# Dividing three PSUM banks differently between transposes and weighted values, in hash-masked attention followed by a mixture of adapters

## The chip, the cores and the metric

The kernel runs on one core of a Trainium2 chip. The core has a matrix engine (TensorE, PE in the profile), three engines for elementwise work (VectorE or DVE, ScalarE or ACT, GpSimd or POOL) and a queue engine for transfers (SyncE or SP). [...] The metric is the time on the device in microseconds (us); less is better.

## The reference

```python
def _attn_ref(q, k, v, proj):                       # q, k, v: (4, 8, 768, 64), proj: (64, 6)
    scale = 1.0 / np.sqrt(D)
    q_bits = (np.einsum('bhsd,dk->bhsk', q, proj) > 0).astype(np.int64)
    k_bits = (np.einsum('bhsd,dk->bhsk', k, proj) > 0).astype(np.int64)
    powers = 2 ** np.arange(n_bits)
    q_bucket = np.sum(q_bits * powers, axis=-1)
    k_bucket = np.sum(k_bits * powers, axis=-1)
    mask = q_bucket[:, :, :, None] == k_bucket[:, :, None, :]
    scores = scale * np.matmul(q, k.transpose(0, 1, 3, 2))
    scores = np.where(mask, scores, -1000000000.0)
    scores = scores - np.max(scores, axis=-1, keepdims=True)
    attn = np.exp(scores)
    attn = attn / (np.sum(attn, axis=-1, keepdims=True) + 1e-09)
    return np.matmul(attn, v)

def _moe_ref(x, w_gate, A, B):                      # x: (3072, 512), 8 experts of rank 16, 2 per row
    logits = x @ w_gate
    topk = np.argpartition(-logits, K, axis=1)[:, :K]
    sel = np.take_along_axis(logits, topk, axis=1)
    sel = sel - sel.max(-1, keepdims=True)
    w = np.exp(sel)
    w /= w.sum(-1, keepdims=True) + 1e-09
    ...
            z = x[mask] @ A[e]
            delta[mask] += w[mask, k, None] * (z @ B[e])
    return x + delta
```

The result of the attention, with its eight heads side by side, is the `x` of the second part.

## The kernel before

**Pairs and slots.** The 32 heads (4 batches of 8) are worked off as 16 pairs of two heads. A pair has 12 times 768 columns of scores of 128 keys each, and these are cut into nine slots of 1,024 columns. In slot s, `score(p, s)` (line 315) computes one group of scores into one of two PSUM buffers of two banks each (`ps_s`), and ScalarE turns it into exponentials in SBUF, P (line 324). This text calls these score s and exp s. The signs of the hash are six more rows of the operands `aug`, so a mask needs no work of its own.

**Order.** Every engine takes its instructions in the order in which the program issues them. That order is written out by hand: `run` (line 587) issues score s of a pair and then, in `pair(p, s)` (line 632), what else belongs to that slot. This work is for three pairs at once:

- For pair p+1 and p+2: `trans` (line 228) brings four 128x128 blocks of q and k into transposed form on TensorE, into a bank of `ps_t`; VectorE (line 244), or ScalarE in some pairs (line 242), copies the bank out to `qkT`. A pair needs three such groups: groups 0 and 1 of pair p+2 in slots 4 and 5 of pair p, group 2 in slot 0 of pair p+1. Behind them GpSimd casts `qkT` to bf16 (`cast`, line 275), and `hash` (line 251) computes the projections on TensorE, again into `ps_t`; VectorE takes their signs (line 260), and SyncE's queue sends these by four small DMAs into `aug` (`sign_dma`, line 163; two of them are issued later, by `hash_b`).
- For pair p-1 and p: `pvmm` (line 333) computes the weighted values, here called pv: six query slices per head, each of six matmuls of 65 columns, all into one bank of `ps_v`. `pv(p,0)` is issued in slots 6, 7 and 8, two slices in each; `pv(p-1,1)` of the pair before in slots 1 and 3, three slices in each. `norm` (line 363) then adds the uniform part that keeps empty buckets defined (line 374), takes the reciprocal of the sums and multiplies (line 379) into `x`; for the second head GpSimd also casts `x` to bf16 (`xb`, line 385). The next pv in the same bank has to wait for that. `uniform` (line 354) computes the uniform part of a pair by one matmul into `ps_t`, copied out by VectorE (line 361). From pair 12 on a matmul with a tiny constant (`eps`, line 340) does this inside the bank of pv.
- `vcast` (line 214) prepares v for pair p+1 on GpSimd. `xturn` (line 443) transposes `xb` by a DMA; in every fourth pair `xtrans` (line 451) does it on TensorE, through a bank of `ps_t`.
- The adapters (MoE) run in `moe_slot` (line 568) from pair 5 on, one to three row slots in a pair: two in pairs 5, 6, 9 and 10, one in pairs 7, 8, 11 and 12, three in 13 and 14. Logits and low-rank products (lz, line 477) come in slots 0 and 1, routing on VectorE in slots 1 to 3, the transpose of the weighted products (`zmtrans`, line 525; its copy zmT is line 534) in slot 4, and `delta` (line 538) from slot 6 on. All of these go through the one bank of `ps_m`.

**Banks.** `ps_s` holds four banks, `ps_t` two, `ps_v` one and `ps_m` one, eight in all. A tile of a pool waits until the tile that had its buffer before has been read for the last time. Some tiles are put into other pools by hand: the second head of pair 14 uses `ps_t` for its pv, and in the last pair, which `last_pair` (line 673) issues in thirds and sixths, `third` and `sixth` alternate between `ps_v` and `ps_t`.

Of the kernel before, what the change touches and what calls it, by code (L numbers as in the profile page):

```python
# [12 lines left out]
F32 = mybir.dt.float32  # L13
# [6 lines left out]
class Emitter:  # L20


    def __init__(self, ctx, tc, q, k, v, proj, w_gate, A, Bm, out):
        self.tc, self.nc = tc, tc.nc
        nc = self.nc
        self.out = out
        B, H, S, D = q.shape
        self.B, self.H, self.S, self.D = B, H, S, D
        self.nbits = proj.shape[1]
        self.E = w_gate.shape[1]  # L30
        self.r = A.shape[2]
        self.Dm = w_gate.shape[0]
        self.P = P = 128
        self.T = S // P
        self.n_pairs = B * H // 2
        self.PPB = H // 2
        self.ER = self.E * self.r
        self.LZ = self.E + self.ER
        T = self.T
        assert (P, T, D, self.nbits, self.Dm, self.ER) == (128, 6, 64, 6, 512, 128)  # L40

        self.nat, self.vn, self.qkT, self.P_, self.pv = {}, {}, {}, {}, {}
        self.x, self.xb, self.xT, self.lz = {}, {}, {}, {}
        self.uni = {}
        self.rt, self.zm, self.zmT, self.acc, self.pvl, self.me, self.gw = {}, {}, {}, {}, {}, {}, {}
        one = lambda n: ctx.enter_context(tc.tile_pool(name=n, bufs=1))
        self.singles = one("singles")
        self.natp = ctx.enter_context(tc.tile_pool(name="natp", bufs=3))
        self.qktp = ctx.enter_context(tc.tile_pool(name="qktp", bufs=2))
        self.sgp = ctx.enter_context(tc.tile_pool(name="sgp", bufs=2))  # L50
        self.pp = ctx.enter_context(tc.tile_pool(name="pp", bufs=2))
        self.xp = ctx.enter_context(tc.tile_pool(name="xp", bufs=2))
        self.accp = ctx.enter_context(tc.tile_pool(name="accp", bufs=3))
        self.smallp = ctx.enter_context(tc.tile_pool(name="smallp", bufs=4))
        ps = lambda n, b: ctx.enter_context(
            tc.tile_pool(name=n, bufs=b, space=bass.MemoryType.PSUM))
        self.ps_s = ps("ps_s", 2)
        self.ps_t = ps("ps_t", 2)
        self.ps_v = ps("ps_v", 1)
        self.ps_m = ps("ps_m", 1)  # L60

        self.q, self.k, self.v, self.proj = q, k, v, proj
        self.w_gate, self.A, self.Bm = w_gate, A, Bm
        self.nD = self.Dm // P


    def prologue(self):
        nc, sg, P, T, D, S = self.nc, self.singles, self.P, self.T, self.D, self.S

        self.pst = sg.tile([P, 6], F32, name="pst")  # L70
        nc.scalar.dma_start(out=self.pst, in_=self.proj.unsqueeze(0).to_broadcast([2, D, 6]))
        nat = self.natp.tile([P, 2, 2, T * D], F32, tag="nat", name="nat0")
        self.nat[0] = nat
        for h in range(2):
            for i, src in enumerate((self.q, self.k)):
                nc.sync.dma_start(out=nat[:, i, h], in_=src[0, h].rearrange("(p t) d -> p (t d)", t=T))
        self.load_qk(1)
        self.load_v(0)

        self.eps = sg.tile([P, P], BF16, name="eps")  # L80
        nc.vector.memset(self.eps, 2.0 ** -56)
        self.ident = sg.tile([P, P], F32, name="ident")
        make_identity(nc, self.ident)
        first = sg.tile([P, 1], F32, name="first")
        nc.scalar.activation(out=first, in_=self.eps[:, 0:1], func=ACT.Exp)
        self.proj2 = sg.tile([P, 32], F32, name="proj2")
        nc.vector.memset(self.proj2, 0.0)

        self.aug = [sg.tile([P, 4, S], BF16, name=f"aug{i}") for i in range(2)]
        for j in range(8):  # L90
            eng = nc.vector if j < 2 else nc.gpsimd
            eng.memset(self.aug[j // 4][64:96, j % 4, :], (1.0, -1.5)[j % 2])
        self.qkT[0] = self.qktp.tile([P, 2 * S], F32, tag="qkT", name="qkT0")
        self.warm(19)
        self.turn0(0, self.ps_s, "s")
        self.half0(0, 0, nc.scalar.copy)
        self.half0(0, 1, nc.scalar.copy)
        self.signs0()
        self.turn0(1, self.ps_t, "t")
        for e in range(2):  # L100
            nc.vector.tensor_copy(out=self.proj2[64 * e:64 * e + 64, e:12:2],
                                  in_=self.pst[64 * e:64 * e + 64, :])
        self.half0(1, 0, nc.gpsimd.tensor_copy)
        self.half0(1, 1, nc.gpsimd.tensor_copy)

        self.vb = []
        for i in range(3):
            a = sg.tile([P, 2, T + 1, D + 1], BF16, name=f"vb{i}")
            nc.gpsimd.memset(a[:, :, 0:T, D:D + 1], 1.0)
            nc.gpsimd.memset(a[:, :, T:T + 1, D:D + 1], float(T))  # L110
            self.vb.append(a)
        self.vcast(0)
        self.ident_bf = sg.tile([P, P], BF16, name="ident_bf")
        nc.gpsimd.tensor_copy(out=self.ident_bf, in_=self.ident)
        self.wa = sg.tile([P, self.nD, self.LZ], BF16, name="wa")
        self.Bcat = sg.tile([self.ER, self.Dm], BF16, name="Bcat")
        self.warm(6)
# [107 lines left out]

    def trans(self, p, g, on_act=False):
        if p >= self.n_pairs:
            return  # L230
        nc, P = self.nc, self.P
        if g == 0:
            self.qkT[p] = self.qktp.tile([P, 2 * self.S], F32, tag="qkT", name=f"qkT{p}")
        ps = self.ps_t.tile([P, 512], F32, tag="t", name=f"tr{p}_{g}")
        for j in range(4):
            idx, u = divmod(4 * g + j, 3)
            nc.tensor.transpose(out=ps[:, j * P:(j + 1) * P],  # L237
                                in_=self.nat[p][:, idx % 2, idx // 2, u * P:(u + 1) * P],
                                identity=self.ident)
        out = self.qkT[p][:, g * 512:(g + 1) * 512]  # L240
        if on_act:
            nc.scalar.mul(out, ps, 2.0 ** -5)
        else:
            nc.vector.tensor_scalar(out=out, in0=ps, scalar1=2.0 ** -5, scalar2=None, op0=ALU.mult)  # L244
# [88 lines left out]
    def pvmm(self, p, h, i0, i1):  # L333
        if p < 0:
            return
        if i0 == 0:
            pool, tag = (self.ps_t, "t") if (p, h) == (self.n_pairs - 2, 1) else (self.ps_v, "v")
            self.pv[p, h] = pool.tile([self.P, self.T, self.D + 1], F32, tag=tag, name=f"pv{p}_{h}")
            if self.uni_pe(p):
                self.nc.tensor.matmul(  # L340
                    out=self.pv[p, h], lhsT=self.eps, start=True, stop=False,
# [46 lines left out]
    def third(self, u, part):  # L388
        nc, P, T, D = self.nc, self.P, self.T, self.D
        p, b = self.n_pairs - 1, self.B - 1  # L390
        if part == 0:
            pool, tag = (self.ps_t, "t") if u == 1 else (self.ps_v, "v")
            pv = pool.tile([P, 2, 2, D + 1], F32, tag=tag, name=f"pvl{u}")
            ri = self.smallp.tile([P, 2, 2], F32, tag="ri", name=f"ril{u}")
            self.pvl[u] = pv, ri
            nc.tensor.matmul(
# [14 lines left out]
    def sixth(self, sl, j0, j1):  # L411
        nc, P, T, D = self.nc, self.P, self.T, self.D
        p, b = self.n_pairs - 1, self.B - 1
        if j0 == 0:
            pool, tag = (self.ps_v, "v") if sl == 4 else (self.ps_t, "t")
            pv = pool.tile([P, 2, D + 1], F32, tag=tag, name=f"pvs{sl}")
            ri = self.smallp.tile([P, 2], F32, tag="ri", name=f"ris{sl}")
            self.pvl[sl] = pv, ri
            nc.tensor.matmul(out=pv, lhsT=self.eps, rhs=self.vb[p % 3][:, :, T, :], start=True, stop=False)
# [183 lines left out]
    def first_pair(self, s):  # L603
# [3 lines left out]
            self.load_v(1)  # L607
            self.load_v(2)
        if s < 3:
            self.trans(1, s)  # L610
        if s == 3:
            self.cast(1, 0)
            self.cast(1, 1)
# [9 lines left out]
            self.trans(2, 0)  # L623
        if s == 7:
            self.pvmm(0, 0, 2, 4)
            self.trans(2, 1)
        if s == 8:
            self.pvmm(0, 0, 4, 6)
            self.load_moe(0)
# [2 lines left out]
    def pair(self, p, s):  # L632
# [2 lines left out]
            self.trans(p + 1, 2)  # L635
            self.load_qk(p + 3, (0,))
        if s == 1:
            self.pvmm(p - 1, 1, 0, 3)
            self.cast(p + 1, 0)
            self.cast(p + 1, 1)  # L640
        if s == 2:
# [2 lines left out]
                self.hash_b(p + 1)  # L644
            self.load_qk(p + 3, (1,))
        if s == 3:
            self.uniform(p)
            self.pvmm(p - 1, 1, 3, 6)
        if s == 4:
            self.norm(p - 1, 1)  # L650
            self.trans(p + 2, 0, on_act=len(self.moe_group(p)[1]) > 1)
        if s == 5:
            if p % self.PPB:
                self.xturn(p - 1)
            if p + 1 < self.n_pairs - 1:
                self.hash_b(p + 1)
            self.vcast(p + 1)
            self.trans(p + 2, 1)
            if p < 4:
                self.load_moe(p + 1)  # L660
            if p == 3:
# [1 line left out]
        if s == 6:  # L663
            self.pvmm(p, 0, 0, 2)
        if s == 7:
            self.pvmm(p, 0, 2, 4)
        if s == 8:
            self.pvmm(p, 0, 4, 6)
            if p % self.PPB == 0:
                self.xtrans(p - 1)  # L670
            self.load_v(p + 3)
# [1 line left out]
    def last_pair(self, p, b):  # L673
# [46 lines left out]
        self.totals(b, t[1])  # L720
        self.delta(b, t[1], 0, by_pool=True)
        self.route_b(b, t[2], sums=False)
        self.zmtrans(b, t[2], on_act=True, bank=one)
        self.sixth_x(5, x)
        self.totals(b, t[2])
        self.delta(b, t[1], 1, by_pool=True)
# [49 lines left out]
```

## Time and profile before

| what | us |
|---|---|
| median of 11 runs | 178.44 (177.79 to 179.54) |
| the profiled execution | 178.51 |
| its span, first to last instruction | 176.7 |

TensorE's granted clock in this execution was 0.983 on average. A pair's length can be read from the starts of its exps. From exp 3 of one pair to exp 3 of the next:

| from pair to pair | adapter slots of the two pairs | us |
|---|---|---|
| 1 to 2, 2 to 3, 3 to 4 | 0, 0 | 8.91, 8.92, 8.92 |
| 4 to 5 | 0, 2 | 9.96 |
| 5 to 6, 9 to 10 | 2, 2 | 9.85, 9.85 |
| 6 to 7, 10 to 11 | 2, 1 | 9.61, 9.61 |
| 7 to 8, 11 to 12 | 1, 1 | 9.71, 9.71 |
| 8 to 9 | 1, 2 | 10.56 |
| 12 to 13 | 1, 3 | 10.25 |
| 13 to 14 | 3, 3 | 10.56 |

Exp 3 of pair 1 starts 22.95 after the first instruction, and exp 3 of pair 14 at 149.34; what comes before and after are the start and the last pair.

How to read the profile's rows: the name on the left of an arrow is written, those on the right are read. On TensorE the rows of matmuls that follow each other overlap, because they are pipelined, and their ends are modelled; how long a step holds the engine is read from its start to the start of the next step. What stands in brackets is the idle time before a row, and the row that ended it.

### The profile page before, as it was taken

The numbers are of one execution on the slowest core, as the hardware profiler recorded it, in microseconds if no ns is written. First come the engines' busy times: TensorE is split into PE (matmuls) and PEld (weight loads), VectorE is DVE, ScalarE is ACT, GpSimd is POOL, SyncE is SP. The second block draws the span as 40 slices with busy tenths as digits, with TensorE's granted clock in tenths as the row PEclk, the third lists the DMA queues.
The fourth block names the chain that finished last, engine by engine and source line by source line (L and its number), as shares of the span: only waits on it lengthen the run. The fifth ranks groups of instructions, "written<-read, shape, count | busy, mean of one in ns | idle before, by whom it ended". The sixth has DMA issues, their size and how long they took to land.

```text
span 176.7 us, 5259 instructions
## 1 busy us (share of the span) xinstructions
PE 162.1 (92%) x2100; PEld 112.7 (64%) x2105; DVE 115.3 (65%) x312; ACT 151.8 (86%) x176; POOL 115.4 (65%) x140
## 2 busy tenths in 40 slices
PE   7989999999999999998989999998999999999750
PEld 6355676767676666666666666666578675687610
DVE  3663674747475686868496686868594776646861
ACT  3578999999999798998998799998999897997760
POOL 8299988787975676666664676666675566620180
PEclk9999999999999999999999999999999999999985
DMA  5936496998997078958864378968965034350036
GB/s 149 344 134 185 153 260 144 170 129 210 121 232 259 5 125 249 192 141 282 137 222 151 111 132 264 171 161 264 131 225 168 4 50 182 41 195 4 2 121 235
DMA packets 30438, 28.51 MB, mean 161 GB/s; under 512 B 15078, under 2 KB 28494, under 8 KB 30414
## 3 DMA queue, kind: packets, MB, share of 16 engines
q1 hardware_dynamic: 25020, 27.38, 58.6%
q0 software_dynamic: 4832, 0.27, 4.6%
q10 hardware_dynamic: 562, 0.53, 0.9%
q8 instruction: 16, 0.26, 0.7%
q14 instruction: 8, 0.07, 0.1%
HBM read 19.42 MB, written 6.29 MB: 145 GB/s over the span
## 4 chain that ended last, share of the span: by engine, by line
PE 69%; DVE 15%; POOL 6%; issue 5%; ACT 2%; DVEq 0%; POOLq 0%; ACTq 0%
PE s L322 27%; PE pv L329 15%; PE tr L237 8%; PE hs L257 7%; PE lz L477 3%; POOL xb L385 2%; PE dl L545 2%; DVE x L379 2%; DVE pv L374 2%; POOL vs L221 2%; DVE sgn L260 2%; DVE zm L510 1%; POOL vb L219 1%; PE warm L184 1%; PE xtp L460 1%
## 5 line engine op out<-in xcount | busy, mean ns | idle before, releaser
L324 ACT ACTIVATE P<-s 128x1024 bf16<-128x1024 f32 x144 | 140.6, 1028 | 12.4 <-PE s L322 11.3
L322 PE MATMUL s<-aug 71*128 71x256 bf16 (+2 forms) x408 | 86.2, 316 | 2.1 <-issue 0.8
L275 POOL CAST aug<-qkT 64x1536 bf16<-64x1536 f32 x30 | 43.8, 1461 | 18.1 <-DVE qkT L244 14.7
L329 PEld LDWEIGHTS <-P 128*128 128x128 bf16 x1080 | 42.1, 97 | 12.5 <-DVE x L379 4.4
L329 PE MATMUL pv<-vb,P 128*128 128x65 bf16 x1080 | 45.2, 194 | 2.7 <-DVE zmT L534 1.7
L322 PEld LDWEIGHTS <-aug 71*128 71x128 bf16 x408 | 33.0, 97 | 21.0 <-issue 10.7
L244 DVE TENSOR_SCALAR qkT<-tr 128x512 f32<-128x512 f32 x40 | 26.9, 682 | 2.3 <-POOL aug L275 1.3
L385 POOL CAST xb<-x 128x768 bf16<-128x768 f32 x15 | 12.3, 822 | 23.5 <-DVE x L379 19.8
L237 PE MATMUL tr<-ident,nat 128*128 128x128 f32 x180 | 27.2, 273 | 0.0
L237 PEld LDWEIGHTS tr<-ident,nat 128*128 128x128 f32 x180 | 21.8, 140 | 4.8 <-issue 0.6
L260 DVE TENSOR_SCALAR sgn<-hs 128x384 bf16<-128x384 f32 x15 | 8.4, 558 | 17.7 <-PE hs L257 16.9
L374 DVE TENSOR_TENSOR pv<-pv,uni 128x390 f32<-128x390 f32 x24 | 13.6, 565 | 9.0 <-PE pv L329 8.7
L553 DVE SCALAR_TENSOR_TENSOR acc<-dl,rt,x 128x512 f32<-128x512 f32 (+1 forms) x21 | 15.0, 720 | 6.7 <-PE dl L545 6.7
L379 DVE TENSOR_TENSOR x<-pv,ri 128x384 f32<-128x384 f32 x30 | 16.7, 557 | 1.0
L221 POOL TENSOR_TENSOR vs<-vn 128x384 f32<-128x384 f32 x16 | 15.9, 992 | 0.0
L219 POOL CAST vb<-vn 128x768 bf16<-128x768 f32 x16 | 13.2, 825 | 0.1
L257 PE MATMUL hs<-qkT,proj 128*32 128x384 f32 x120 | 12.8, 498 | 0.0
L551 POOL TENSOR_TENSOR acc<-tmp,x 128x512 f32<-128x512 f32 x4 | 5.0, 1264 | 8.8 <-ACT tmp L550 8.8
L477 PE MATMUL lz<-wa,xT 128*128 128x136 bf16 x96 | 9.3, 223 | 0.6 <-ACT xT L462 0.6
L545 PE MATMUL dl<-Bcat,zmT 128*128 128x512 bf16 x19 | 7.7, 404 | 1.0 <-ACT zmT L534 0.8
L224 POOL TENSOR_TENSOR vb<-vs,vs 128x128 bf16<-128x128 f32 x16 | 7.3, 457 | 1.3
L223 POOL TENSOR_TENSOR vs<-vs 128x128 f32<-128x128 f32 x16 | 7.3, 454 | 1.3
(73 smaller groups left out, 118.9 us busy)
## 6 DMA issues: line engine op xcount, KB each, us to landing
vn<-in_v_dram SPq DMA_DIRECT2D x16, 384.0 KB
nat<-in_q_dram SPq DMA_DIRECT2D x15, 384.0 KB
nat<-in_k_dram SPq DMA_DIRECT2D x15, 384.0 KB
out_dram<-acc SPq DMA_DIRECT2D x4, 512.0 KB
out_dram<-acc SPq DMA_DIRECT2D x8, 256.0 KB
out_dram<-acc SPq DMA_DIRECT2D x2, 768.0 KB
aug<-sgn SPq DMA_DIRECT2D x60, 9.0 KB
nat<-in_q_dram SPq DMA_DIRECT2D x2, 192.0 KB
```

The costliest lines, as they stand in the source:

```text
L221: nc.gpsimd.tensor_add(out=s3, in0=vn[:, :, 0:3, :], in1=vn[:, :, 3:6, :])
L237: nc.tensor.transpose(out=ps[:, j * P:(j + 1) * P], in_=self.nat[p][:, idx % 2, idx // 2, u * P:(u + 1) * P], identity=self.ident)
L244: nc.vector.tensor_scalar(out=out, in0=ps, scalar1=2.0 ** -5, scalar2=None, op0=ALU.mult)
L257: nc.tensor.matmul(out=ps[32 * j:32 * j + 32, :], lhsT=self.proj2, rhs=self.qkT[p][:, j * 384:(j + 1) * 384], start=True, stop=True)
L275: self.nc.gpsimd.tensor_copy(out=self.aug[p % 2][0:64, :, e * n:(e + 1) * n], in_=self.qkT[p][64 * e:64 * e + 64, :].rearrange("p (j c) -> ...
L322: nc.tensor.matmul(out=ps[:, o:o + n], lhsT=aug[0:71, 2 * h + 1, kt * P:(kt + 1) * P], rhs=q, start=True, stop=True)
L324: nc.scalar.activation(out=self.P_[p][:, s * 1024:(s + 1) * 1024], in_=ps, func=ACT.Exp, scale=128.0)
L329: self.nc.tensor.matmul(out=pv, lhsT=self.p_at(p, h, kt, i), rhs=self.vb[p % 3][:, h, self.slot(kt), :], start=(start and kt == 0), stop=( ...
L374: nc.vector.tensor_tensor(out=pv[:, 0:T, :], in0=pv[:, 0:T, :], in1=self.uni[p][:, h:h + 1, :].to_broadcast([P, T, D + 1]), op=ALU.add)
L379: nc.vector.tensor_tensor(out=self.x[b][:, :, c:c + D].rearrange("p (u e) d -> p e u d", e=2), in0=pv[:, 0:T, 0:D].rearrange("p (e u) d -> ...
L385: nc.gpsimd.tensor_copy(out=self.xb[b][:, hp], in_=self.x[b][:, :, hp * P:(hp + 1) * P])
L553: nc.vector.scalar_tensor_tensor(out=acc[:, i, c], in0=ps[:, c], scalar=self.rt[b, slots][:, i:i + 1], in1=self.x[b][:, slots[i], c], op0= ...
```

## The change

The pools are divided anew: one bank for transposes (`ps_t`), two for weighted values (`ps_v`). Then the work is moved between the slots of a pair:

- pv(p-1,1) in slots 1, 3 and 4, two slices each, in place of slots 1 and 3, three each; pv(p,0) in slots 6, 7 and 8 with two, one and three slices in place of two each.
- `uniform` from slot 3 to slot 4, behind pv; `hash_b` from slot 5 to slot 4; the norm of pv(p-1,1) from slot 4 to slot 5.
- The transposes of groups 0 and 1 from slots 4 and 5 to slots 5 and 7; `xturn` from slot 5 to slot 7.
- In the first pair, which has no adapters yet, three groups of transposes use `ps_m`, and the prologue's second turn uses `ps_v`.
- The tiles that were put into `ps_t` for want of a second bank in `ps_v` are in `ps_v` now, and the last `zmtrans` is in `ps_m`.

What is computed stays the same, and so does the number of instructions of every kind on the compute engines.

```diff
@@ pools
-        self.ps_t = ps("ps_t", 2)
-        self.ps_v = ps("ps_v", 1)
+        self.ps_t = ps("ps_t", 1)
+        self.ps_v = ps("ps_v", 2)
@@ prologue
-        self.turn0(1, self.ps_t, "t")
+        self.turn0(1, self.ps_v, "v")
@@ trans
-    def trans(self, p, g, on_act=False):
+    def trans(self, p, g, on_act=False, bank=None):
...
-        ps = self.ps_t.tile([P, 512], F32, tag="t", name=f"tr{p}_{g}")
+        pool, tag = bank or (self.ps_t, "t")
+        ps = pool.tile([P, 512], F32, tag=tag, name=f"tr{p}_{g}")
@@ pvmm
-            pool, tag = (self.ps_t, "t") if (p, h) == (self.n_pairs - 2, 1) else (self.ps_v, "v")
-            self.pv[p, h] = pool.tile([self.P, self.T, self.D + 1], F32, tag=tag, name=f"pv{p}_{h}")
+            self.pv[p, h] = self.ps_v.tile([self.P, self.T, self.D + 1], F32, tag="v", name=f"pv{p}_{h}")
@@ third
-            pool, tag = (self.ps_t, "t") if u == 1 else (self.ps_v, "v")
-            pv = pool.tile([P, 2, 2, D + 1], F32, tag=tag, name=f"pvl{u}")
+            pv = self.ps_v.tile([P, 2, 2, D + 1], F32, tag="v", name=f"pvl{u}")
@@ sixth
-            pool, tag = (self.ps_v, "v") if sl == 4 else (self.ps_t, "t")
-            pv = pool.tile([P, 2, D + 1], F32, tag=tag, name=f"pvs{sl}")
+            pv = self.ps_v.tile([P, 2, D + 1], F32, tag="v", name=f"pvs{sl}")
@@ first_pair
-            self.trans(1, s)
+            self.trans(1, s, bank=None if s == 1 else (self.ps_m, "m"))
...
-            self.trans(2, 1)
+            self.trans(2, 1, bank=(self.ps_m, "m"))
@@ pair
         if s == 1:
-            self.pvmm(p - 1, 1, 0, 3)
+            self.pvmm(p - 1, 1, 0, 2)
...
         if s == 3:
+            self.pvmm(p - 1, 1, 2, 4)
+        if s == 4:
+            self.pvmm(p - 1, 1, 4, 6)
             self.uniform(p)
-            self.pvmm(p - 1, 1, 3, 6)
-        if s == 4:
-            self.norm(p - 1, 1)
-            self.trans(p + 2, 0, on_act=len(self.moe_group(p)[1]) > 1)
-        if s == 5:
-            if p % self.PPB:
-                self.xturn(p - 1)
             if p + 1 < self.n_pairs - 1:
                 self.hash_b(p + 1)
+        if s == 5:
+            self.norm(p - 1, 1)
             self.vcast(p + 1)
-            self.trans(p + 2, 1)
+            self.trans(p + 2, 0, on_act=len(self.moe_group(p)[1]) > 1)
...
         if s == 7:
-            self.pvmm(p, 0, 2, 4)
+            if p % self.PPB:
+                self.xturn(p - 1)
+            self.trans(p + 2, 1)
+            self.pvmm(p, 0, 2, 3)
         if s == 8:
-            self.pvmm(p, 0, 4, 6)
+            self.pvmm(p, 0, 3, 6)
@@ last_pair
-        self.zmtrans(b, t[2], on_act=True, bank=one)
+        self.zmtrans(b, t[2], on_act=True)
```

## The prediction

> **What bounds the kernel now.** I read the page's first part, then ScalarE's timeline, then TensorE's and VectorE's timelines through single head pairs. The page:
>
> ```profile
> PE 162.1 (92%) x2100; PEld 112.7 (64%) x2105; DVE 115.3 (65%) x312; ACT 151.8 (86%) x176; POOL 115.4 (65%) x140
> L324 ACT ACTIVATE P<-s 128x1024 bf16<-128x1024 f32 x144 | 140.6, 1028 | 12.4 <-PE s L322 11.3
> ```
>
> Exps fill ScalarE; what it waits for is scores. Its timeline (start, length, idle before) shows where:
>
> ```profile
> 31.86 8.62 ACT L324 ACTIVATE P<-s 128x1024 bf16<-128x1024 f32 x9 [0.30 <-PE s L322]
> ...
> 58.33 1.02 ACT L324 ACTIVATE P<-s 128x1024 bf16<-128x1024 f32 x1 [0.78 <-PE s L322]
> ...
> 83.49 5.03 ACT L324 ACTIVATE P<-s 128x1024 bf16<-128x1024 f32 x5 [0.47 <-PE s L322]
> ```
>
> The first is exp 3 of pair 2, behind hash and slot 1's weighted values; the second exp 2 of pair 5; the third exp 7 of pair 7. TensorE's rows, pair 7 and then pair 5's one line:
>
> ```profile
> 77.16 0.60 PE L322 MATMUL s<-aug 71*128 71x256 bf16 x3
> 77.68 0.85 PE L257 MATMUL hs<-qkT,proj 128*32 128x384 f32 x8
> 78.47 0.61 PE L322 MATMUL s<-aug 71*128 71x512 bf16 x3
> 78.91 0.22 PE L359 MATMUL un<-vb,eps 128*128 128x130 bf16 x1
> 78.97 0.71 PE L329 MATMUL pv<-vb,P 128*128 128x65 bf16 x18
> 79.52 0.60 PE L322 MATMUL s<-aug 71*128 71x512 bf16 x2
> 79.95 0.60 PE L237 MATMUL tr<-ident,nat 128*128 128x128 f32 x4
> 80.39 0.22 PE L531 MATMUL ztp<-ident_bf,zm 128*128 128x128 bf16 x1
> 80.45 0.60 PE L322 MATMUL s<-aug 71*128 71x256 bf16 x3
> 80.88 0.60 PE L237 MATMUL tr<-ident,nat 128*128 128x128 f32 x4
> 81.32 0.60 PE L322 MATMUL s<-aug 71*128 71x512 bf16 x3
> 82.49 0.53 PE L329 MATMUL pv<-vb,P 128*128 128x65 bf16 x12 [0.57 <-DVE zmT L534]
> 82.86 0.60 PE L322 MATMUL s<-aug 71*128 71x512 bf16 x2
> ...
> 56.90 0.72 PE L329 MATMUL pv<-vb,P 128*128 128x65 bf16 x18 [0.41 <-DVE x L379]
> ```
>
> Rows overlap, so a step's cost is start to next start: score 0.44 (0.52 ahead of the hash), hash 0.79, four transposes 0.44, 18 weighted-value matmuls 0.55 (0.183 a query slice), 12 of them 0.37, uniform 0.06, one adapter transpose 0.06. Likewise, elsewhere: logits of one slot 0.24, delta 0.22, the six bf16 transposes 0.33, an eps matmul (pairs 12 up) 0.17. Nearly no gap is left: a pair without MoE takes 8.92 us from exp 3 to exp 3, with 0.44 of TensorE waiting. [...] The starts allow 0.44; I follow them.
>
> **Rules of my sums**, all from rows: an exp starts 0.64 after its score, and 0.91 after the exp before at the earliest; score s+2 starts 0.05 after exp s ends (score 0: 0.26), an exp lasting 1.02 to 1.05. Walking the old order of a pair without MoE by these gives 8.9; the trace has 8.92.
>
> **Part 1, weighted values get two banks.** Slot 1's pv(p-1,1) no longer waits for norm(p-1,0) to empty the one bank: 0.31 in pair 1, 0.57 in pairs 5 and 9 (starts 55.89 to 56.90, less 0.44). With one bank, norm(p-1,1) had to be over before slot 6; now it may come later.
>
> **Part 2, norm(p-1,1) in slot 5 behind the adapter copy zmT.** Delta at slot 6 waits for zmT, which VectorE runs behind that norm (0.59+0.23+0.47=1.3) and a transpose copy (0.60). By starts the stall is 0.52 in pairs 7, 8, 11 (81.32 to 82.49, less score 0.44 and delta 0.22), 0.27 in pair 12, 0.20 in the two-slot pairs 5, 6, 9, 10. In the new order zmT follows the uniform copy directly, 0.8 before delta needs it: all gone. Moved with norm, on POOL: the xb cast (0.82) and vcast (2.7) behind it, about a slot later, ending near 7.3 after score 3 (8.2 in pairs 1 to 3, with load_moe's 0.9); the casts behind them wait for slot 0's transposes until about 7.9 anyway. If that cover went, a late cast would first meet score 0 of the next pair, nine slots on.
>
> **Part 3, 2+2+2 and 2+1+3.** One slice (0.18) leaves the stretch before the hash; 24 matmuls instead of 18 follow it, where a slot has 0.91 and score+pv needs 0.81. Uniform in slot 4 is behind them.
>
> **Part 4, SP.** hash_b's two sign DMAs (0.8 each to issue) go from slot 5 to 4, the DMA transpose (1.26) from slot 5 to 7, past them, behind it the vn load. The signs are needed at score 4 of the next pair, xT at the tightest behind score 5 of the last pair, seven slots later: cost zero. xT's landing has no row; between 0 and, if it took more than those 6 us, the excess. I take 0.
>
> **Part 5, one bank for transposes, hash, uniform, xtrans.** This adds waits; all PE work queues behind them. [...] Walk of pair 7, score 3 at 0: pv 0.44, score 0.81, pv 1.25, uniform 1.61, adapter transpose 1.67, score 5 1.73, transposes 2.16, score 6 2.63 (waits for exp 4), delta 3.07, pv 3.28, score 7 3.65. VectorE: uniform copy 1.87 (0.26 after its matmul, as 78.91 to 79.17), zmT 2.08, norm 2.21, transpose copy 3.52 to 4.20. Slot 7's transposes, ready at 4.09, start at 4.23: **wait 0.14**. Then pv 4.67, score 8 4.85, pv 5.29, score 0 5.84, transposes 6.27, logits 6.71, score 1 6.95, pv 7.38, score 2 7.75, hash 8.28, score 3 **9.06**; the old interval is 9.71.
> Cost bounds of that wait: 0 (copy on ScalarE, as in pairs 5, 6, 9, 10, 13) to 0.74 (one delta op of VectorE ahead); a wait gains nothing; the rows above give 0.11 to 0.14, which I take.
> xtrans in pairs 4, 8, 12: its copy ends 1.09 after its first matmul (54.45 to 55.54), the next transposes are due at 0.77: **wait 0.35** each. In pair 12 no norm wait goes in exchange (that norm lacks the add), so it loses.
> Pair 0: uniform directly behind the hash now waits for the sign copy (end 15.63, and 0.05): 15.68 against 14.93, **0.75**. Slack further on (pair 1's 0.31 wait, its slice) leaves 0.24.
>
> **The other walks**, score 3 at 0, by the same costs. *No MoE*: score 5 1.72, score 6 2.63, score 7 3.55, transposes due 3.99 and held to 4.10, score 8 4.72, pv 5.16, score 0 5.71, score 1 6.58, pv 7.02, score 2 held by exp 0 to 7.42, hash 7.95, score 3 8.74. *4 to 5*: the same to 5.71, then xtrans, score 0 6.04, transposes held to 6.83, logits 7.27, score 1 7.50, pv 7.94, logits 8.31, score 2 8.54, hash 9.07, score 3 9.86. *8 to 9*: pair 7's walk to 5.84, then as 4 to 5: 9.98. *Two slots*: score 5 1.78, score 6 2.65, delta 3.09, pv 3.30, score 7 3.67, transposes 4.10 (copy on ScalarE, no wait), pv 4.54, delta 4.72, score 8 4.95, pv 5.38, score 0 held by exp 7 to 6.07, transposes 6.50, logits 6.94, score 1 7.18, pv 7.61, logits 7.98, score 2 8.21, hash 8.74, score 3 9.53; into a one-slot pair one logits group less, 9.29. *12 to 13*, with eps, xtrans and three logits groups: 10.42. *13 to 14*: delta's waits for its own bank stay, 10.46.
>
> **Sum**, old minus new from exp 3 to exp 3: start to pair 1 -0.24; three without MoE, 8.92 to 8.74, +0.54; 4 to 5, 9.96 to 9.86, +0.10; 5 to 6 and 9 to 10, 9.85 to 9.53, +0.64; 6 to 7 and 10 to 11, 9.61 to 9.29, +0.64; 7 to 8 and 11 to 12, 9.71 to 9.06, +1.30; 8 to 9, 10.56 to 9.98, +0.58; 12 to 13, 10.25 to 10.42, -0.17; 13 to 14, +0.10; pair 14 to score 0 of pair 15 (no transposes; zmT early again, a stall of 0.36) +0.37. Last pair: its pv tiles alternated between two banks and still do; zmtrans goes to ps_m, emptied by a copy over 1 us earlier (ScalarE, 168.49, for a transpose at 169.89): 0.
> Total 3.9. The walks forget small jitters; I take 3.8: the profiled execution's 178.51 becomes **174.7**. It lies 0.07 above the median of the runs, 178.44.
>
> **Rivals.** *Only the named waits go*: if slot 7, now 0.44+0.18+0.22 beside the score, lets no slice gain through, there remain pair 1, 5, 9 (0.31+2×0.57), zmT (3×0.52+0.27+4×0.20+0.36), less 3×0.35 and 0.75: 2.6, so 175.9. For it: in two-slot pairs TensorE waits just 0.45 of 9.85. Against: slots 3 to 5 got lighter. *Slower*: the slot 7 transposes wait on VectorE behind norm. The mechanism decides from 0.3 more per pair over 13 pairs, 3.9. If a delta op of 0.74 stood before the slot 5 copy in the eight pairs 5 to 12 and jitter put 0.2 on the rest, 6 to 7 us go: 181. Against it: that copy comes before delta in VectorE's order. *Hidden anyway*: ScalarE's pace and the hash stretch (score 0.52, hash 0.79, score 0.64, after 1.08 for an exp: 3.03 of exp 0 to exp 3's 3.2) swallow it: 178.4.
>
> **Chances.** Forecast 0.60, named waits only 0.19, hidden 0.08, slower 0.13. Range 173.5 to 178.1: below, the walk's 3.9 with both 0.35 and 0.75 waits half as large; above, four fifths reach it. Within 0.3% (0.5 us) is what no change looks like. Faster 0.79, same 0.07, slower 0.14.
>
> **What would show it.** Right: no DVE zmT and no DVE x ahead of weighted values on TensorE; exp 3's idle of 0.30 near 0.12; exp 7's 0.47 gone; new waits of about 0.1 before slot 7's transposes on VectorE's copy, 0.35 behind xtrans, 0.7 in pair 0. Wrong: transposes waiting over 0.4 in every pair, or delta in slot 7 waiting for its bank.

## The result and the profile after

| | before | after |
|---|---|---|
| median (runs) | 178.50 (47) | 176.34 (12, 175.46 to 178.73) |
| the profiled execution | 178.51 | 176.48 |
| its span | 176.7 | 174.7 |

The ratio after to before is 0.9875, with a 95% interval of 0.9853 to 0.9898: the change saves about 2.2 us in the medians and 2.03 between the two profiled executions. The forecast was 3.8, so little more than half of it came. The ratio is taken over executions within 1.5% of the fastest; two of the twelve after, at 178.60 and 178.73, are left out of it.

The page of the kernel after, its first part, and its groups for exps, weighted values and transposes (busy time and mean of one, idle time before them and what ended it); the last two rows are those of before for weighted values and transposes. Line numbers differ from those of before by up to two.

```profile
PE 162.2 (93%) x2100; PEld 112.1 (64%) x2105; DVE 116.1 (66%) x312; ACT 150.7 (86%) x176; POOL 115.4 (66%) x140
L325 ACT ACTIVATE P<-s 128x1024 bf16<-128x1024 f32 x144 | 139.7, 1030 | 11.6 <-PE s L323 10.0
L330 PE MATMUL pv<-vb,P 128*128 128x65 bf16 x1080 | 47.5, 194 | 0.2
L238 PEld LDWEIGHTS tr<-ident,nat 128*128 128x128 f32 x180 | 20.2, 140 | 10.0 <-DVE qkT L245 3.1
...
L329 PE MATMUL pv<-vb,P 128*128 128x65 bf16 x1080 | 45.2, 194 | 2.7 <-DVE zmT L534 1.7 <-DVE x L379 1.0
L237 PEld LDWEIGHTS tr<-ident,nat 128*128 128x128 f32 x180 | 21.8, 140 | 4.8 <-issue 0.6
```

ScalarE's wait for scores fell from 11.3 to 10.0. The weighted values wait for nothing any more (0.2 in all, where 2.7 stood before). The transposes now wait, as announced, on VectorE's copies of the one bank; the wait shows at the weight load (PEld), which comes first. Its 10.0 is not lost time of TensorE as it stands: the matmuls of these transposes had 0.6 of idle before them. ScalarE's timeline at the places that answer to those shown of before (start, length, idle before):

```profile
32.50 8.69 ACT L325 ACTIVATE P<-s 128x1024 bf16<-128x1024 f32 x9 [0.17 <-PE s L323]
...
57.88 2.07 ACT L325 ACTIVATE P<-s 128x1024 bf16<-128x1024 f32 x2 [0.46 <-PE s L323]
...
79.09 4.74 ACT L325 ACTIVATE P<-s 128x1024 bf16<-128x1024 f32 x5
84.00 4.03 ACT L325 ACTIVATE P<-s 128x1024 bf16<-128x1024 f32 x4 [0.17 <-PE s L323]
```

Exp 3 of pair 2 has 0.17 of idle ahead of it instead of 0.30. The 0.46 ahead of exp 1 of pair 5 is the wait behind xtrans; the 0.78 ahead of exp 2 is gone. From exp 3 of pair 7 five exps run without a gap, and exp 7's 0.47 is gone; ahead of exp 8 there is a new 0.17, behind slot 7's transposes. TensorE's timeline of pair 7, and then two weight loads of transposes and the uniform's copy:

```profile
78.44 0.61 PE L323 MATMUL s<-aug 71*128 71x512 bf16 x3
78.89 0.53 PE L330 MATMUL pv<-vb,P 128*128 128x65 bf16 x12
79.26 0.60 PE L323 MATMUL s<-aug 71*128 71x512 bf16 x2
79.69 0.53 PE L330 MATMUL pv<-vb,P 128*128 128x65 bf16 x12
80.06 0.22 PE L359 MATMUL un<-vb,eps 128*128 128x130 bf16 x1
80.12 0.22 PE L529 MATMUL ztp<-ident_bf,zm 128*128 128x128 bf16 x1
80.17 0.60 PE L323 MATMUL s<-aug 71*128 71x256 bf16 x3
80.67 0.66 PE L238 MATMUL tr<-ident,nat 128*128 128x128 f32 x4
81.16 0.60 PE L323 MATMUL s<-aug 71*128 71x512 bf16 x3
81.81 0.53 PE L330 MATMUL pv<-vb,P 128*128 128x65 bf16 x12
82.18 0.60 PE L323 MATMUL s<-aug 71*128 71x512 bf16 x2
82.69 0.66 PE L238 MATMUL tr<-ident,nat 128*128 128x128 f32 x4
...
80.32 0.29 DVE L361 COPY uni<-un 128x130 f32<-128x130 f32 x1 [0.46 <-PE un L359]
80.66 0.42 PEld L238 LDWEIGHTS tr<-ident,nat 128*128 128x128 f32 x4 [0.28 <-DVE uni L361]
84.68 0.47 PEld L238 LDWEIGHTS tr<-ident,nat 128*128 128x128 f32 x4
```

Up to score 5 (1.73 after score 3) this is the walk of the prediction to 0.01. Then slot 5's transposes start 0.50 behind it (80.17 to 80.67) instead of 0.44, and last 0.49 to the next score (80.67 to 81.16) instead of 0.44: they waited 0.06 for the uniform's copy (it ends at 80.61, just when they are due), and four transposes that start after a wait take 0.055 longer (the *restart*). The weight loads fit that: after the wait the first starts with the transposes (80.66 and 80.67), while ahead of slot 0's transposes at 84.79, which take 0.44, it starts 0.11 earlier. So score 6 starts 2.72 after score 3, where the walk had 2.63. Slot 7's transposes, ready at 82.62, start at 82.69 and again take 0.49. Delta in slot 6 has no matmul record here, but from score 6 to pv there are 0.65, its own 0.22 and the score's 0.44, so nothing waits there. The intervals from exp 3 to exp 3:

| from pair to pair | before | forecast | after |
|---|---|---|---|
| start to 1 | 22.95 | 23.19 | 23.20 |
| 1 to 2 | 8.91 | 8.74 | **9.31** |
| 2 to 3, 3 to 4 | 8.92, 8.92 | 8.74 | 8.86, 8.87 |
| 4 to 5 | 9.96 | 9.86 | 10.02 |
| 5 to 6, 9 to 10 | 9.85 | 9.53 | 9.54 |
| 6 to 7, 10 to 11 | 9.61 | 9.29 | 9.30 |
| 7 to 8, 11 to 12 | 9.71 | 9.06 | 9.14 |
| 8 to 9 | 10.56 | 9.98 | 10.15 |
| 12 to 13 | 10.25 | 10.42 | 10.50 |
| 13 to 14 | 10.56 | 10.46 | 10.74 |
| 14 to 15 | 9.18 | 8.81 | 8.93 |
| 15 to the end | 18.19 | 18.19 | 18.17 |

The first row agrees by luck in part: exp 0 of pair 0 starts at 9.01 before and 8.96 after, and anywhere from 8.20 to 9.32 in the profiles of this study. From there to exp 3 of pair 1 the change took 0.30 more, where 0.24 was forecast. The two waits that were forecast on a single user of the bank, first in pair 0 (the second two rows are before), then behind xtrans:

```profile
14.04 0.85 PE L258 MATMUL hs<-qkT,proj 128*32 128x384 f32 x8
15.57 0.23 PE L359 MATMUL un<-vb,eps 128*128 128x130 bf16 x1 [0.68 <-DVE sgn L261]
...
14.15 0.85 PE L257 MATMUL hs<-qkT,proj 128*32 128x384 f32 x8
14.93 0.23 PE L359 MATMUL un<-vb,eps 128*128 128x130 bf16 x1
...
55.70 0.60 PE L323 MATMUL s<-aug 71*128 71x512 bf16 x3
56.52 0.66 PE L238 MATMUL tr<-ident,nat 128*128 128x128 f32 x4 [0.22 <-DVE xT L460]
```

### The profile page after: what moved, and what is told of

Same layout as the page of the kernel before. It is cut to its first block, busy times and chain, and to the rows that moved or that the text cites. A ratio compares the mean times of both kernels' runs of the same rounds, so it can differ in the third digit from the quotient of the medians.

```text
span 174.7 us, 5249 instructions
## 1 busy us (share of the span) xinstructions
PE 162.2 (93%) x2100; PEld 112.1 (64%) x2105; DVE 116.1 (66%) x312; ACT 150.7 (86%) x176; POOL 115.4 (66%) x140
## 3 DMA queue, kind: packets, MB, share of 16 engines
q0 software_dynamic: 4832, 0.27, 4.7%
## 4 chain that ended last, share of the span: by engine, by line
PE 79%; DVE 7%; POOL 5%; issue 3%; ACT 2%; POOLq 1%; ACTq 0%; DVEq 0%
PE s L323 32%; PE pv L330 17%; PE tr L238 12%; PE hs L258 7%; PE lz L475 4%; PE dl L543 1%; POOL xb L385 1%; PE warm L184 1%; PE xtp L458 1%; DVE xT L460 1%; POOL vs L221 1%; ACT P L325 1%; PE trf L125 1%; POOL vb L219 1%; PE hsd L139 1%
## 5 line engine op out<-in xcount | busy, mean ns | idle before, releaser
L330 PEld LDWEIGHTS <-P 128*128 128x128 bf16 x1080 | 44.9, 98 | 11.3
L330 PE MATMUL pv<-vb,P 128*128 128x65 bf16 x1080 | 47.5, 194 | 0.2
L245 DVE TENSOR_SCALAR qkT<-tr 128x512 f32<-128x512 f32 x40 | 27.5, 686 | 8.9 <-PE tr L238 8.4
L238 PE MATMUL tr<-ident,nat 128*128 128x128 f32 x180 | 28.3, 280 | 0.6 <-DVE xT L460 0.6
L238 PEld LDWEIGHTS tr<-ident,nat 128*128 128x128 f32 x180 | 20.2, 140 | 10.0 <-DVE qkT L245 3.1
L543 PE MATMUL dl<-Bcat,zmT 128*128 128x512 bf16 x19 | 7.2, 381 | 1.1 <-ACT zmT L532 0.8
L361 DVE COPY uni<-un 128x130 f32<-128x130 f32 x12 | 3.5, 294 | 7.2 <-PE un L359 7.2
```

Source lines behind the costliest of these rows:

```text
L238: nc.tensor.transpose(out=ps[:, j * P:(j + 1) * P], in_=self.nat[p][:, idx % 2, idx // 2, u * P:(u + 1) * P], identity=self.ident)
L330: self.nc.tensor.matmul(out=pv, lhsT=self.p_at(p, h, kt, i), rhs=self.vb[p % 3][:, h, self.slot(kt), :], start=(start and kt == 0), stop=( ...
```

## The experiments

Theory: the walk, that is the prediction's sum of steps along a pair. Two banks for weighted values and the later norm take waits away, one bank for transposes adds some, and each shows in the interval of its pairs. Rivals: only one half of the change matters, or the smaller pieces alone give the gain. The experiments start from the kernel after unless it says otherwise.

**The two halves alone.** `banks_only` has the new banks with the body of `pair` of before; `order_only` the new order with the banks of before (`ps_t` 2, `ps_v` 1, and the tiles that were put into other pools). The edits in short:

```diff
 banks_only: pools, prologue, first_pair, third, sixth as in after
-    def pair(self, p, s):        # after
+    def pair(self, p, s):        # before
 order_only: pair as in after
-        self.ps_t = ps("ps_t", 1)
+        self.ps_t = ps("ps_t", 2)
-        self.ps_v = ps("ps_v", 2)
+        self.ps_v = ps("ps_v", 1)
```

> The new banks with the old order of a pair's slots. Walk theory (the two halves need each other): uniform stands right behind the hash and waits about 0.3 us for the sign copy, group 1's transposes in slot 5 wait 0.5 us for group 0's copy behind the norm in the pairs where VectorE makes it, and zmT keeps its place behind the norm; against that only the waits of 0.3 and twice 0.57 for pv's bank go. Slower than before: 180 to 183 us. Rival (the second bank for weighted values brings the gain, the order only repairs the transposes): 176.5 to 178 us.

> The new order with the old banks (two for transposes, one for weighted values). Walk theory: pv(p,0) in slot 6 must now wait for the norm issued in slot 5, 0.2 to 0.4 us in every pair, and pv(p,1) in slot 1 for the norm of slot 0; zmT's stalls stay gone. 177.5 to 180 us, on TensorE a wait for DVE x ahead of pv in nearly every pair. Rival (the order alone brings the gain, and one bank for pv is enough): 175.5 to 176.5 us, since the waits on the single transpose bank are gone too.

Measured: `banks_only` 193.67, ratio 1.082 (1.073 to 1.091); `order_only` 179.61, ratio 1.007 (1.004 to 1.010). Neither half gives a gain. A group of `banks_only` (transposes) and one of `order_only` (weighted values):

```profile
L238 PE MATMUL tr<-ident,nat 128*128 128x128 f32 x180 | 29.0, 284 | 10.9 <-DVE qkT L245 7.2 <-ACT qkT L243 3.0 <-DVE xT L460 0.6
```

```profile
L330 PE MATMUL pv<-vb,P 128*128 128x65 bf16 x1080 | 47.7, 194 | 5.0 <-DVE x L380 5.0
```

With one bank and transposes in neighbouring slots TensorE stands 10.9 us before them; a pair without MoE takes 10.11 to 10.12. I had the direction and a fifth of the size. (In two of its four executions, the profiled one among them, 1 to 2 us more go with a halved clock, which is told of at the end; the fastest took 192.00.) With the new order and one bank for weighted values these wait 5.0 us for norm, which now comes a slot later. The two halves only work together.

**The norm ahead of zmT again** (Part 2 undone).

```diff
 slot 4:
             self.uniform(p)
+            self.norm(p - 1, 1)
 slot 5:
-            self.norm(p - 1, 1)
```

> The changed kernel, but the norm of pv(p-1,1) issued in slot 4 ahead of the adapter copy zmT. Walk theory: delta in slot 6 waits again, 0.5 to 0.6 us in pairs 5 to 12, at most 0.2 in 13 and 14, so 2.5 to 4.5 us slower than the changed kernel: 179 to 181 us. Rival (delta's wait is hidden, since TensorE makes up for it before the next exp is due): within 0.7 us of the changed kernel.

Measured: 180.77, ratio 1.013 (1.008 to 1.018); its profiled execution 179.53, 3.05 above that of after. TensorE in `norm_first`, slots 6 to 7 of pair 7:

```profile
81.75 0.60 PE L323 MATMUL s<-aug 71*128 71x512 bf16 x3
82.91 0.53 PE L330 MATMUL pv<-vb,P 128*128 128x65 bf16 x12 [0.56 <-DVE zmT L532]
```

From score 6 to pv 1.16 instead of 0.65: delta (whose record is missing) waits for zmT again, as it did before the change. The eight intervals from pairs 5 to 12 take 0.33 to 0.51 more each (5 to 6: 10.04; 7 to 8: 9.52), 3.47 in all; pairs 2 to 4 stay at 8.86, and 1 to 2 is 8.86 too, 0.45 less than in after. Without Part 2 the rest of the change loses time.

**Three and three slices instead of 2+2+2** (part of Part 3 undone).

```diff
-            self.pvmm(p - 1, 1, 0, 2)
+            self.pvmm(p - 1, 1, 0, 3)
-            self.pvmm(p - 1, 1, 2, 4)
+            self.pvmm(p - 1, 1, 3, 6)
-            self.pvmm(p - 1, 1, 4, 6)
```

> The changed kernel, but pv(p-1,1) in two pieces of three slices in slots 1 and 3 as before the change. Walk theory: 0.18 us more ahead of the hash counts only where ScalarE and not TensorE sets the pair, that is in pairs 1 to 4, so 0.3 to 0.8 us slower than the changed kernel. Rival (the smaller pieces away from the hash are what the change gains by): 0.18 us in each of 14 pairs and more, 2 to 3 us slower.

Measured: 177.86, ratio 0.994 (0.991 to 0.998), between the two. The profiled execution has the halved clock up to 21.77, so only intervals behind it are compared. Where the loss lies was the surprise: pairs without MoE take 8.83, 0.03 *less* than after, while intervals from two-slot pairs are 0.25 longer (5 to 6: 9.79), 12 to 13 takes 0.25 and 13 to 14 0.18 more. From pair 2 to the end these and smaller ones sum up to 1.57. In one-slot pairs the slice costs 0.03 (7 to 8: 9.17). My reading: in pairs without MoE the slice that leaves the stretch before the hash comes back in slot 4, ahead of the uniform, whose copy then holds slot 5's transposes (`un3`, next, supports that); in two-slot pairs TensorE is full and the slice counts (argued, not tested).

**Other banks for single users.** `xtp_m` puts xtrans into `ps_m`, `un0_m` the uniform of pair 0; `un3` issues the uniform at the end of slot 3 in every pair; `combo` does all three.

```diff
 xtp_m:
-                self.xtrans(p - 1)
+                self.xtrans(p - 1, bank=(self.ps_m, "m"))
 un0_m:
-            self.uniform(0)
+            self.uniform(0, bank=(self.ps_m, "m"))
 un3:
             self.pvmm(p - 1, 1, 2, 4)
+            self.uniform(p)
 ...
             self.pvmm(p - 1, 1, 4, 6)
-            self.uniform(p)
```

> The changed kernel, but xtrans in pairs 4, 8 and 12 goes through ps_m, which is empty there, and not through the one transpose bank. Theory (the single bank makes slot 0's transposes wait for xT's copy, 0.38 us and 0.05 for the restart, and TensorE never makes it up): exp 3 to exp 3 from 10.02, 10.15 and 10.50 to about 9.6, 9.75 and 10.1, in all 1.2 us less than the changed kernel, 175.1 us. Rival (the logits need the same copy and would wait instead, so the wait only moves): 176.0 to 176.5 us.

> The changed kernel, but the first pair's uniform goes through ps_m. Theory (TensorE stands still for 0.75 us between hash and uniform, behind it all scores of the pair, and only part is made up): exp 5 of pair 0 from 16.28 to about 15.6, exp 3 of pair 1 from 23.20 to 22.7, the kernel 0.3 to 0.7 us shorter. That idle stretch also stands just ahead of the 6.8 us in which some profiles of such kernels grant half the clock (15.3 to 22.1); if it is the cause, the executions that are some 3 us longer become rare. Rival (the wait is made up in pair 1): within 0.2 us of the changed kernel, and half the clock as often as with it.

> The changed kernel, but uniform stands at the end of slot 3 and not of slot 4. Theory (the single bank's waits of slots 5 and 7 come from uniform's copy, and from the norm that queues behind it on VectorE): both waits go, exp 3 to exp 3 of a pair without adapters from 8.86 to 8.7, of one-slot pairs from 9.14 to 9.0, two-slot pairs within 0.1 of 9.54; in all 0.6 to 1.0 us less than the changed kernel. Rival (ScalarE's pace and the stretch around the hash set these pairs, and the waits on the bank are hidden): within 0.2 us.

> All three of these edits together. If the three waits on the single bank are what is missing of the forecast gain, their gains add: 2.0 to 2.6 us less than the changed kernel, 173.7 to 174.4 us, with no wait on the transpose bank above 0.1 us in any pair. If they only lie beside ScalarE's pace, less than 1 us goes.

Measured: `xtp_m` 175.48, ratio 0.981 (0.977 to 0.984); 4 to 5 went to 9.61, 8 to 9 to 9.74, 12 to 13 to 10.06, each about 0.42 less. `un0_m` 175.35, ratio 0.983 (0.980 to 0.986); from exp 4 to exp 5 of pair 0 1.38 instead of 2.13, and from exp 0 to exp 3 of pair 1 13.53 instead of 14.24: little of that wait was made up.

`un3` 178.02, ratio 1.000 (0.996 to 1.003): a miss. Its pairs without MoE took 8.66, as expected (0.20 less than after), but 5 to 6 took 9.97. VectorE and TensorE in `un3`, pair 7:

```profile
79.64 0.29 DVE L361 COPY uni<-un 128x130 f32<-128x130 f32 x1 [0.38 <-PE un L359]
79.84 0.22 DVE L506 SCALAR_TENSOR_TENSOR gw<-lz,top,e 128x8 f32<-128x8 f32 x1
80.10 0.29 DVE L508 TENSOR_TENSOR zm<-lz,gw 128x128 bf16<-128x128 f32 x1
```

```profile
79.87 0.53 PE L330 MATMUL pv<-vb,P 128*128 128x65 bf16 x12
80.44 0.23 PE L529 MATMUL ztp<-ident_bf,zm 128*128 128x128 bf16 x1
80.51 0.60 PE L323 MATMUL s<-aug 71*128 71x256 bf16 x3
```

The uniform's copy now stands ahead of the routing's two operations, zm comes later, and its transpose, due 0.37 behind pv, comes 0.57 behind it; all TensorE work queues there. I had looked at TensorE only.

`combo` 175.70, ratio 0.984 (0.981 to 0.988): `un3`'s loss is in it, and a wait in pair 2 that I had not known. TensorE in `combo`:

```profile
26.36 0.71 PE L330 MATMUL pv<-vb,P 128*128 128x65 bf16 x18
28.60 0.59 PE L323 MATMUL s<-aug 71*128 71x512 bf16 x3 [1.54 <-DMA aug<-sgn]
```

Score 0 of pair 2 waits for the signs of its hash (1-to-2 interval 10.36). By the transfer records, 44 of the 48 sign packets of that pair had ended by 27.72, and the last four by 28.90. In after the same score starts late too:

```profile
27.79 0.71 PE L330 MATMUL pv<-vb,P 128*128 128x65 bf16 x18
28.78 0.60 PE L323 MATMUL s<-aug 71*128 71x512 bf16 x3 [0.28 <-POOL vs L221]
```

The row names GpSimd's vs, but that can't be it: in `xtp_m` the same score started 0.4 before that vs ended. The last four of 48 sign packets end 0.31 after this start in after, 0.26 in `un0_m` and 0.30 in `combo`, the three that are late by 0.44 or more; in `un3` and `best_load` (below), late by 0.35 and 0.36, they end some 0.2 after it. But a packet's record that ends behind the start can't be the release itself, and score 0 of pair 3 in after starts on time with its last four packets ending 0.7 later. So that the signs hold this score is shown by the row in `combo` and argued for the others. Of after's 9.31, the lateness is the excess over 8.86.

**What holds the signs up, and the best of all.** `un0_late` is `un0_m` with the adapter weights' loads (`load_moe`) moved from pairs 0 to 3 to pairs 2 and 3. `best` adds `xtp_m`'s edit, and the uniform at the end of slot 3 where no adapter runs; `best_load` is `best` with the loads of after; `best_gap` is `best` with pair 0's uniform in `ps_t`.

```diff
 un0_late (first_pair, slot 8; pair):
-            self.load_moe(0)
-            self.load_moe(1)
...
-            if p < 4:
-                self.load_moe(p + 1)
-            if p == 3:
-                self.load_moe(5)
+            if p in (2, 3):
+                self.load_moe(2 * p - 4)
+                self.load_moe(2 * p - 3)
             self.load_v(p + 3)
+            if p == 3:
+                self.load_moe(4)
+                self.load_moe(5)
 best, besides:
             self.pvmm(p - 1, 1, 2, 4)
+            if p < 5:
+                self.uniform(p)
...
             self.pvmm(p - 1, 1, 4, 6)
-            self.uniform(p)
+            if p >= 5:
+                self.uniform(p)
```

> The kernel after with pair 0's uniform in ps_m (the earlier run un0_m), and load_moe's loads issued in pairs 2 and 3 instead of pairs 0 to 3. My theory of the 9.31 us from exp 3 of pair 1 to exp 3 of pair 2 (8.74 forecast, 8.86 in the later pairs without MoE): score 0 of pair 2 waits for the four sign transfers of its hash, which are in the DMA engines at the same time as load_moe's transfers of 16 and 32 B packets. Without those: 1 to 2 at 8.83 to 8.90, and 0.4 to 0.5 us less than un0_m in the whole, 174.9 if un0_m is 175.35. First rival: the large loads of q, k and v of the start hold the signs up, and load_moe has no part: 1 to 2 stays within 0.1 of 9.31 and the time at 175.35. Second rival: the loads put later collide with the signs of pairs 3 and 4: 1 to 2 at 8.87, but 2 to 3, 3 to 4 or 4 to 5 longer by as much, and no change of the time.

> un0_late with, besides, xtrans through ps_m (earlier run xtp_m: 0.41, 0.41 and 0.44 less in pairs 4, 8 and 12, 0.86 in the time) and uniform at the end of slot 3 in pairs 1 to 4 alone, where no routing of the adapters stands behind it on VectorE (earlier run un3: 8.66 instead of 8.86 in these pairs, but about 0.4 more in pairs 5 to 12). My theory, that these are separate waits whose gains add up: 174.9 of un0_late, less 0.86, less about 3 x 0.2 and up to 0.2 in 4 to 5: 173.3 to 173.7; pairs 1 to 4 at 8.66, 5 to 6 at 9.54, 8 to 9 at 9.74. Rival: a wait that is taken away in one pair comes back as another one (as score 0 of pair 2 did for the signs in the earlier run of three edits together): 174.3 or more.

> best with load_moe's loads in pairs 0 to 3 again, as in after. If these loads are what holds the signs of pair 2 up: exp 0 of pair 2 comes 0.3 to 1.4 us later than its place in best (exp 0 of pair 1 to exp 0 of pair 2 was 8.66 in best and 9.31 to 10.36 in the kernels where it was late), and the median is 0.3 to 0.8 above best's 173.16. If the landing of the signs merely varies from one execution to the next whatever load_moe does: 8.66 or late in the profile, as it falls, and a median within 0.2 of best's.

> best with pair 0's uniform in ps_t again, which puts 0.75 us of waiting for the sign copy behind the first hash. My theory: this gap, beyond its 0.75 us, lets the clock of TensorE be halved for one stretch of about 6.8 us in some executions, which makes those 3 us longer and lowers the mean granted clock from 0.98 to about 0.965. So far that mean clock came in 16 of 54 executions of kernels with this wait and in none of 34 of kernels of this study without it. Then: median 173.9 to 174.6 and one or more executions of this kernel at 176 to 177 with a mean clock of 0.96 to 0.97 (with a chance of 0.3 each, 9 times in 10 at least one among six). Rival: the halved clock is an accident of the chip, not of the gap: all executions of this kernel within 1.5 us of each other, or best_load, which has no such wait, shows it just as often.

Measured:

| kernel | median | ratio (95%) | 1 to 2 |
|---|---|---|---|
| un0_late | 175.29 | 0.981 (0.977 to 0.985) | 8.86 |
| best | 173.16 | 0.970 (0.966 to 0.974) | 8.67 |
| best_load | 173.91 | 0.975 (0.972 to 0.978) | 9.03 |
| best_gap | 174.17 | 0.981 (0.976 to 0.987) | 8.66 |

`best` is the fastest, 5.3 us below before, and its gains did add up (173.3 to 173.7 was expected). ScalarE's timeline of `best`, from exp 3 of pair 2 on, where nine exps take 8.49 instead of 8.69:

```profile
30.64 8.49 ACT L325 ACTIVATE P<-s 128x1024 bf16<-128x1024 f32 x9 [0.17 <-PE s L323]
```

On the loads the runs don't agree. Without them in the start the late score of pair 2 did not appear in three profiles of three; with them it appeared in five of eight, and not in before, `banks_only` and `pv33` either, of which the last two had been delayed by the halved clock. `best_load` is 0.75 slower than `best`, but in its profile, 1.06 longer, exp 0 of pair 0 already starts 0.88 later, ahead of all these loads, and only 0.36 lies in 1 to 2. `un0_late` is only 0.06 faster than `un0_m`, where I expected 0.45. And in `best_gap` the lateness comes back elsewhere: 4 to 5 takes 9.77 instead of `best`'s 9.42, score 0 of pair 5 waits for signs, and 3,264 of the 4,832 packets of GpSimd's transfers, which bring these loads, start between 49 and 54.

```profile
54.66 0.33 PEld L323 LDWEIGHTS <-aug 71*128 71x128 bf16 x3 [0.39 <-DMA aug<-sgn]
```

So late signs came only where these loads ran, and not each time; that the loads make them late is supported, not shown, and its size isn't settled. The four late packets are as many as there are sign transfers (four, of twelve packets of 768 B each), one of each perhaps; why they come late was not found.

## Why the prediction was right, and where its sizes were off

Direction, places and most mechanisms were right; the gain was 2.03 where the walk's sum gave 3.86 (put as 3.9, and taken as 3.8).

**Part 1** (two banks for weighted values): as said. No wait of them on norm is left, and `order_only` shows 5.0 us of it with one bank.

**Part 2** (norm behind zmT): as said, and undoing it costs 3.47 in pairs 5 to 12. The two-slot pairs were forecast to 0.01. No interval shows a loss from the delayed work of GpSimd.

**Part 3** (pieces): right as to sign, wrong as to place. By `pv33` a slice is worth 0.25 in two-slot pairs, 0.03 in one-slot pairs and nothing in pairs without MoE. There the forecast was 8.74 and the result 8.86, since the step counted slot 5's transposes as never waiting for the uniform's copy; with the uniform a slot earlier `un3` and `best` take 8.66.

**Part 4** (SP, cost zero): no new wait on xT or on the second pair of signs showed; these moves were not undone by themselves. But score 0 of pair 2, whose signs I did not price, was late: 0.45 of the 0.57 missed in 1 to 2. That is one profile's reading, as `norm_first`, `xtp_m` and `order_only` did not have it.

**Part 5** (one bank): the waits are where they were said to be, pair 0's at its size (1.53 from hash to uniform, 0.78 before: 0.75). Mis-sized: each wait costs 0.055 more than its length, as the transposes restart; slot 5's wait for the uniform's copy was put at zero (0.06 and 0.055); slot 7's was 0.07 and 0.055 against 0.14 in pair 7, which is near, and 0.14 and 0.055 against 0.11 in pairs without MoE; xtrans cost 0.38 and 0.055 against 0.35. `xtp_m` gives back 0.42 a time, so that term is shown.

The terms that were off, after less forecast: 1 to 2 0.57; 2 to 4 0.25; 4 to 5 0.16; 7 to 8 and 11 to 12 0.16; 8 to 9 0.17; 12 to 13 0.08; 13 to 14 0.28; 14 to 15 0.12; the four two-slot intervals 0.04. Sum 1.83, and 3.86 less 1.83 is the 2.03 that was measured. In 13 to 14 delta's third run waits 0.29 for its own bank (141.90 to 142.74, less 0.55) instead of 0.19 before (143.70 to 144.26, less 0.37): 0.10 of the 0.28. The rest of it, and the 0.12 of the last pair, were not traced further.

**Rivals.** *Only the named waits go* gave 175.9, closer to the 176.48 than my 174.7. Its mechanism, that no slice gain comes through, holds in pairs without MoE and nearly in one-slot pairs (0.57 gained in 7 to 8, against 0.52 by the named wait and 0.65 by the walk), but not in two-slot pairs (0.31 gained in 5 to 6, against 0.20 and 0.32; a slice counts 0.25 there by `pv33`). It has no restarts and no wait on the uniform's copy either, so its misses in both directions cancel in part: in 4 to 5 it has a gain of 0.22, and 0.06 was lost. *Slower*: slot 7's transposes were never held over 0.14. *Hidden anyway*: no; `norm_first` moves the time by the waits it brings back. Two slots apart a wait for the transposes' bank cost 0.12 to 0.19 with its restart, where the walk had 0.11 to 0.14; one slot apart TensorE stood 10.9 us before the transposes, and `banks_only` was 15 us slower than before.

## What to carry to other kernels

Count a bank by the spacing of its users: with copies of 0.68 us two slots apart (2.02 and 2.10 us by the starts 80.67, 82.69 and 84.79 in pair 7) one bank cost 0.12 to 0.19 a wait, and the second bank was worth more with the weighted values, whose norm takes 1.3 us. Change order and banks together, as each alone lost time here. For every operation that is moved, write down what stands behind it on *each* engine, since the uniform's copy of 0.29 us on VectorE cost more in `un3` than TensorE gained. Price a wait with its restart, and give each small transfer that a score waits for a landing time in the sum, with a spread.

## What the hardware showed that was not expected

**A wait of 0.75 us, and in some executions a halved clock of TensorE behind it.** In `pv33` the wait of pair 0 was followed by this (first the row that ends the wait; then stretches of the profile: length, busy time of PE, PEld, DVE, ACT and POOL, granted clock, DMA share, GB/s):

```profile
14.95 0.29 PE L359 MATMUL un<-vb,eps 128*128 128x130 bf16 x1 [0.68 <-DVE sgn L261]
...
8.00:14.94 6.94, 5.42 (x37) 2.60 (x34) 3.60 (x8) 4.90 (x5) 6.31 (x15) 1.00 0.64 216
14.94:21.77 6.83, 6.82 (x48) 4.93 (x49) 1.67 (x3) 2.96 (x3) 5.83 (x7) 0.50 0.51 160
21.77:30.00 8.23, 8.16 (x111) 5.63 (x109) 4.70 (x11) 7.91 (x9) 4.29 (x4) 1.00 0.78 145
11.53:14.94 3.41, 2.09 (x15) 0.50 (x12) 1.25 (x2) 2.73 (x3) 3.19 (x6) 1.00 0.55 167
```

For 6.83 us the clock is 0.50, with TensorE busy all the time; `banks_only` has the same stretch (15.25 to 22.08). Executions whose mean clock is 0.96 to 0.97 are mostly 2 to 3 us longer than the others of their kernel. Of the kernels with this wait in pair 0, `best_gap` left aside, 16 of 54 executions had such a mean clock, and none of 38 of the kernels of this study without it. (Six more of the 54, at 0.973 to 0.976 and 1.1 to 1.8 us longer, are not counted.) `best_gap`, which puts the wait back into `best`, had it in 2 of 6 (176.44 and 176.47, clock 0.963; the others 173.93 to 174.18). That the wait makes it more frequent is thereby shown, by counts. That it is the only cause is not: before has no such wait, and of its 64 executions beside the experiments two had 0.971 and 0.972 and took 180.66 and 181.25, where the median was 178.48; there is no profile of these two.

Why it comes in some executions only is not shown. In `pv33` TensorE was busy 5.42 of the 6.94 us before the clock fell, and 2.09 of the last 3.41 (half as long as the halved stretch; the last row): a wait of 0.68 in a thinly filled stretch was followed by the half clock. `banks_only` has 2.09 there too. How full the stretch is doesn't decide alone: of 3.41 us that hold the wait, `best_gap`'s profile, which kept its clock, has 2.26 (12.71 to 16.12), but `combo`'s, which kept it as well, only 1.87 around its wait of 1.54 (25.26 to 28.67). What decides stays open.
